# Unused bf16 matmuls in TensorE's idle stretches, one-hot tables with the tile innermost, and a first half of 256 tokens, in an attention and mixture-of-experts kernel

## The chip, the core and the metric

The kernel runs on one core of a Trainium2 chip. The metric is the device time of one execution in microseconds (us). Below, TensorE is also called PE (matmuls) and PEld (its weight loads), VectorE DVE, ScalarE ACT, GpSimd POOL and SyncE SP, as in the profile.

## What is computed

Three stages follow each other. Nothing but the attention result links the first to the second, and `x` links the second to the third.

```python
# 8 batches, 8 heads, 576 tokens, 64 wide: 4608 tokens of 512
kv  = einsum('bhsd,bhse->bhde', k, v)
out = einsum('bhsd,bhde->bhse', q, kv)
x   = out / sqrt(mean(out*out, -1) + 1e-6) * g_norm
# routing: 4608 tokens, 8 experts, 576 tokens each, best logit first
logits = x @ w_gate
for idx in argsort(-logits.flatten()):
    tok, e = idx // 8, idx % 8
    if assigned[tok] < 0 and counts[e] < 576:
        assigned[tok] = e; counts[e] += 1
x[mask_e] = relu(x[mask_e] @ w1[e]) @ w2[e]      # for each expert e
h = max(x @ m1, x @ m2, x @ m3); result = h @ w_out
```

## The kernel before, in words

**Attention** (lines 76 to 262 and the loop at L425). Four pairs of batches, `bp` 0 to 3. `load` (L80) issues the pair's inputs on SP's queue: `kt` and `vt` in two parts (token tiles 0 to 4, "a", and 5 to 8, "b"), then `qt`; for the first pair each part of k and v comes in two halves of 256 columns. `kv` (L169) multiplies k and v in float32 for four pairs of heads `hp`; a 128x128 float32 matmul leaves two records in the trace. `bd_t` and `bd_w` (L187, L194) build a block matrix that also carries the gate weights, and `o_tile` (L203) multiplies one tile of 128 queries by it; ACT takes the squares (L219) and copies the product to `y` (L220), DVE sums the squares (L221). `norm_a` and `norm_b` (L224, L231) make the norm and the logits `L` for three tiles at a time. `pre` (L302) turns the logits of all 9 tiles of a pair into the best expert `oh`, a key `H`, and a table `G` of key against 63 thresholds (L325); `pre_mm` (L333) counts with it on TensorE (L337).

**First route** (`phase(0)`, L636). `top_search` (L524) narrows a threshold seven times: 36 small matmuls count (L555), `narrow` (L526) sends the result to all partitions by one matmul (L531), and DVE builds the next table (L552). After it L716 sums the counts of each expert, `finish` (L568) numbers the chosen tokens: prefix sums (L572 to L581), then the position of each token as `hi` and `ri` (L595, L596), two one-hot tables `q` (L603) and `w` (L609), and W2, which is `q` times the partition's number (ACT, L605) and times the tile's number (POOL, L606). 36 matmuls (L615) over the tiles and four more (L629) give the list of tokens `IDX`. `gather` (L799) fetches their rows from DRAM in five tiles by POOL's queue, `trans` (L809) transposes a tile on TensorE and writes its high part by ACT (L821) and its low part by DVE (L822) to `X`.

**Experts** (loop at L881). Per expert: 8 blocks `f` of the first weight, each for two halves of 288 tokens (`hf`, HS), three matmuls per product (`mm3`, L826 to L828: high x high, low x high, high x low); then the second weight; then the third layer. `advance` (L785) loads the weights and splits them into `ring` (ACT L341, POOL L342). `tick` (L852) runs after each half: one piece of a decoder for the third layer's weights (DVE L368, L370; POOL L372, L386) while expert 0 runs, and one step of the next expert's route, so the routes of experts 1 to 7 (`phase(p)`, the same `finish`, a search on ACT and DVE at L484) run beside the matmuls. `drain` (L865) ends the route before the next gather.

The order on each engine is the order of the code (a manual schedule): an instruction that waits holds back all behind it on its engine.

Of the kernel before, what the change touches and what calls it, by code (L numbers as in the profile page):

```python
# [32 lines left out]
J0 = 63  # L33
# [3 lines left out]
def body(ctx: ExitStack, tc: tile.TileContext, qx, kx, vx, g, wg, w1, w2, w123, wo, out):  # L37
# [13 lines left out]
    SEL = consts.tile([32, 224], BF, name="SEL")  # L51
    iot18 = consts.tile([128, 18], BF, name="iot18")
    onec = consts.tile([128, NT], F32, name="onec")
# [3 lines left out]
    tri = consts.tile([128, 128], BF, name="tri")  # L57
    iot = consts.tile([128, 32], BF, name="iot")
    BM = consts.tile([96, 3, E], F32, name="BM")
# [44 lines left out]
    for s in range(2):  # L104
# [12 lines left out]
                   allow_small_or_imprecise_dtypes=True)  # L117
    nc.vector.tensor_copy(iot, d1[:, :32])
    nc.vector.tensor_copy(iot18, d1[:, :18])
    nc.gpsimd.memset(SEL, 0.0)  # L120
# [78 lines left out]

    Y = {}  # L200
    SS = {}

    def o_tile(c):  # L203
        bp, ci = divmod(c, TP)
        gi = ci % 3
        if gi == 0:
            Y[0] = aw.tile([128, 3, NH // 2, 144], F32, name="y", bufs=3)
            SS[0] = aw.tile([128, 3, NH], F32, name="ss")
        po = aps.tile([128, 2, 512], F32, name="o", bufs=2)
        o = int(ci >= CA)  # L210
        parts = [(0, 128, 0 if ci < 4 else 1)] if ci != 4 else [(0, 64, 0), (64, 128, 1)]
        for p0, p1, r in parts:
            for hp in range(NH // 2):
                nc.tensor.matmul(po[p0:p1, hp // 2, (hp % 2) * 144:(hp % 2) * 144 + 144],  # L214
                                 QT[bp, o][:, hp, (ci - o * CA) * 128 + p0:(ci - o * CA) * 128 + p1], BD[r][:, hp, :],
                                 start=True, stop=True)
        pv = po[:, :, 0:288].rearrange("p a (b x) -> p a b x", b=2)
        sq = aw.tile([128, 2, 2, 128], F32, name="sq", bufs=4)
        nc.scalar.activation(sq, pv[:, :, :, 0:128], AF.Square)  # L219
        nc.scalar.copy(Y[0][:, gi].rearrange("p (a b) x -> p a (b x)", a=2), po[:, :, 0:288])  # L220
        nc.vector.tensor_reduce(SS[0][:, gi], sq.rearrange("p a b (h d) -> p (a b h) d", d=D),  # L221
                                axis=AX, op=OP.add)
# [79 lines left out]
    def pre(c0, n):  # L302
# [9 lines left out]
        sf = aw.tile([128, n], F32, name="kf")  # L312
        G = aw.tile([128, n, J0], BF, name="G", bufs=2)
        nc.vector.tensor_reduce(best, V.rearrange("p e c -> p c e"), axis=AX, op=OP.max)
# [110 lines left out]
    for bp in range(NP):  # L425
# [15 lines left out]
        for ci in range(TP):  # L441
# [12 lines left out]
            if ci == 5:  # L454
                for _ in range(3):
                    norm_x()
        if bp == NP - 1:
            lds.close()
            w3p = ctx.enter_context(tc.tile_pool(name="w3p", bufs=1, side="right"))
            es = ExitStack()  # L460
            early = es.enter_context(tc.tile_pool(name="early", bufs=1, side="right"))
            for i in ORDER[:9]:
                load64(i)
            x_store(36)
        norm_b()
        pre(t0, TP)
        while XQ:
# [100 lines left out]
    def finish(p, A, TIE):  # L568
# [7 lines left out]
        yield  # L576
        yield
        po = rps.tile([128, 512], F32, name="rps")
        nc.tensor.matmul(po[:, 0:1], tri, tots[:, 0:1], start=True, stop=True)
        nc.tensor.matmul(po[:, 1:2], tri, tots[:, 1:2], start=True, stop=False)  # L580
        nc.tensor.matmul(po[:, 1:2], ones, tots[:, 0:1], start=False, stop=True)  # L581
        of = rt.tile([128, 3], F32, name="of")
        cm = rt.tile([128, NT], F32, name="cm")
# [13 lines left out]
        yield kp  # L597
        W2 = rt.tile([128, 36, 36], BF, name="W1", bufs=2).rearrange("p c (a b) -> p c a b", b=2)
        w = rt.tile([128, 36, 36], BF, name="W1", bufs=2)[:, :, 0:32]
        q = rt.tile([128, NT, 18], BF, name="q", tag="KT0")  # L600
        R = rt.tile([32, 20, 2], BF, name="R")
        nc.gpsimd.memset(R, 0.0)
        nc.vector.tensor_tensor(q, hi[:, :, None].to_broadcast([128, NT, 18]),  # L603
                                iot18[:, None, :].to_broadcast([128, NT, 18]), op=OP.is_equal)
        nc.scalar.activation(W2[:, :, :, 0], q, AF.Copy, scale=tp)  # L605
        nc.gpsimd.tensor_mul(W2[:, :, :, 1], q, iotc[:, :, None].to_broadcast([128, NT, 18]))  # L606
        yield
        for i in (0, 18):
            nc.vector.tensor_tensor(w[:, i:i + 18], ri[:, i:i + 18, None].to_broadcast([128, 18, 32]),  # L609
                                    iot[:, None, :].to_broadcast([128, 18, 32]), op=OP.is_equal)  # L610
            yield
        yield
# [5 lines left out]
        pv = pi[0:32, 0:36].rearrange("p (a b) -> p a b", b=2)  # L618
        if o:
# [257 lines left out]
    w_load()  # L877
    for c in range(3):
        trans(0, c)
    bg_piece(1)  # L880
    for p in range(E):  # L881
# [3 lines left out]
        for f in range(8):  # L885
# [7 lines left out]
            for hf in range(2):  # L893
                cs = slice(hf * HS, hf * HS + HS)
                if p == 0 and f == 0 and hf:
                    trans(0, 3)
                    trans(0, 4)
# [3 lines left out]
                for k in range(4):  # L901
                    mm3(ps[:, :HS], w, slice(k * 128, k * 128 + 128), X[:, k], cs, k == 0, k == 3)
                nc.scalar.activation(h[:, 0, cs], ps[:, :HS], AF.Relu)
                if p or f or hf:
                    tick(2)
                nc.vector.scalar_tensor_tensor(h[:, 1, cs], ps[:, :HS], 0.0, h[:, 0, cs],  # L906
                                               op0=OP.max, op1=OP.subtract)
# [117 lines left out]
```

## Time and profile before

| | us |
|---|---|
| median of 3 runs (lowest, highest) | 1288.56 (1285.23, 1289.71) |
| the profiled execution | 1291.65 |
| its span, first to last instruction | 1289.9 |
| TensorE busy with matmuls | 1206.7 (94%) |
| VectorE, ScalarE, GpSimd busy | 640.2, 491.6, 446.1 |
| mean granted TensorE clock | 0.963 |

The profiled execution is 3.1 us over the median. Slices of the span tell the stages: attention reaches to about 116 us, the first route to about 159 us, the first expert to about 323 us, and the other seven take some 138 us each. In a row of the timeline stand the start, the time from the first to the last of a group (in us), the engine, the line, the operation, output and inputs with shapes, and in brackets the idle time of the engine before it and what ended it. A matmul's duration contains its pipeline; how fast matmuls follow each other is read from starts.

### The profile page before, as it was taken

Reading aid. Unit: us, or ns where it says so; the run is one execution under the profiler, and the core shown is the slowest. Engines: PE = TensorE matmul, PEld = TensorE weight load, DVE = VectorE, ACT = ScalarE, POOL = GpSimd, SP = SyncE. Lnnn points to the kernel's source line nnn. Section 1 sums busy time; section 2 is a strip of 40 time slices with the busy share of each in tenths; the row PEclk is TensorE's granted clock in tenths of the full one; section 3 lists DMA queues with packets and bytes.
Section 4 is the critical chain, followed back from the end, with each engine's and each line's share of the span. In section 5 each row is a group of like instructions: output and inputs, shape, how many; then the busy total and the mean of one; then the engine's idle time right before and its main releaser. Section 6 shows DMA issues by size and latency. Waiting matters only on the chain.

```text
span 1289.9 us, 23164 instructions
## 1 busy us (share of the span) xinstructions
PE 1206.7 (94%) x8814; PEld 1143.6 (89%) x8814; DVE 640.2 (50%) x2017; ACT 491.6 (38%) x1214; POOL 446.1 (35%) x503
## 2 busy tenths in 40 slices
PE   7996386898999999999999999999999999999997
PEld 6886286888899989998999999998999899989995
DVE  2676559985466427652775157625763321122110
ACT  1556336752364125422552155314631331133110
POOL 0342158645531325132412352234213361134121
PEclk9998568898999999999999999999999999999998
DMA  9778722511330313121321133113302152013201
GB/s 327 301 274 334 281 75 83 180 50 58 108 114 26 99 27 122 66 75 47 109 75 58 42 116 98 58 42 96 110 32 69 53 165 94 2 50 123 66 1 41
DMA packets 52031, 133.63 MB, mean 104 GB/s; under 512 B 5840, under 2 KB 10448, under 8 KB 50384
## 3 DMA queue, kind: packets, MB, share of 16 engines
q1 hardware_dynamic: 44672, 109.07, 25.4%
q0 software_dynamic: 6944, 23.07, 5.3%
q8 instruction: 69, 1.13, 0.4%
q14 instruction: 42, 0.34, 0.1%
q10 hardware_dynamic: 304, 0.02, 0.0%
HBM read 110.12 MB, written 22.02 MB: 102 GB/s over the span
## 4 chain that ended last, share of the span: by engine, by line
PE 73%; DVE 13%; issue 5%; ACT 5%; POOL 2%; DMA 1%; POOLq 0%; ACTq 0%; SPq 0%; DVEq 0%
PE mm L826 18%; PE mm L827 17%; PE mm L828 17%; PE kv L179 4%; ACT W L492 3%; PE mm L971 3%; PE mm L973 3%; PE mm L972 3%; DVE T L512 3%; PE o L214 3%; PE tp L815 1%; DVE w L370 1%; DVE H L906 1%; PE rps L615 1%; DVE an L507 1%
## 5 line engine op out<-in xcount | busy, mean ns | idle before, releaser
L826 PE MATMUL mm<-X,w 128*128 128x288 f32 x1152 | 347.4, 302 | 0.0
L827 PE MATMUL mm<-X,w 128*128 128x288 f32 x1152 | 342.4, 297 | 5.0 <-POOL w L386 5.0
L828 PE MATMUL mm<-X,w 128*128 128x288 f32 x1152 | 341.8, 297 | 0.0
L342 POOL TENSOR_TENSOR ring<-raw,ring 128x512 fp32r<-128x512 f32 x128 | 167.8, 1313 | 244.5 <-ACT ring L341 228.4
L827 PEld LDWEIGHTS mm<-X,w 128*128 128x128 f32 x1152 | 218.3, 189 | 5.5 <-POOL w L386 5.5
L948 POOL TENSOR_TENSOR H<-t,H 128x288 fp32r<-128x288 f32 x96 | 78.8, 821 | 410.3 <-ACT H L947 410.2
L826 PEld LDWEIGHTS mm<-X,w 128*128 128x128 f32 x1152 | 218.5, 190 | 0.4
L828 PEld LDWEIGHTS mm<-X,w 128*128 128x128 f32 x1152 | 217.9, 189 | 0.0
L946 DVE TENSOR_TENSOR t<-mm,t 128x288 f32<-128x288 f32 x192 | 87.0, 453 | 171.6 <-PE mm L828 171.3
L826 PE MATMUL mm<-X,ring 128*128 128x288 f32 x512 | 157.2, 307 | 2.3 <-ACT X L821 1.3
L826 PE MATMUL mm<-H,ring 128*128 128x288 f32 x512 | 156.7, 306 | 0.0
L827 PE MATMUL mm<-X,ring 128*128 128x288 f32 x512 | 153.7, 300 | 0.8 <-POOL ring L342 0.8
L828 PE MATMUL mm<-X,ring 128*128 128x288 f32 x512 | 153.8, 300 | 0.0
L827 PE MATMUL mm<-H,ring 128*128 128x288 f32 x512 | 152.2, 297 | 0.0
L828 PE MATMUL mm<-H,ring 128*128 128x288 f32 x512 | 152.1, 297 | 0.0
L492 ACT ACTIVATE W<-KT,T 96x384 bf16<-96x384 f32 x168 | 102.1, 608 | 103.6 <-DVE T L512 103.5
L947 ACT CAST H<-t 128x288 fp32r<-128x288 f32 x96 | 41.3, 430 | 262.0 <-DVE t L946 262.0
L826 PEld LDWEIGHTS mm<-X,ring 128*128 128x128 f32 x512 | 99.2, 194 | 3.6 <-ACT X L821 2.1
L827 PEld LDWEIGHTS mm<-X,ring 128*128 128x128 f32 x512 | 98.9, 193 | 1.2 <-POOL ring L342 1.2
L828 PEld LDWEIGHTS mm<-X,ring 128*128 128x128 f32 x512 | 98.7, 193 | 0.3 <-DVE X L822 0.3
L826 PEld LDWEIGHTS mm<-H,ring 128*128 128x128 f32 x512 | 98.0, 191 | 0.0
L827 PEld LDWEIGHTS mm<-H,ring 128*128 128x128 f32 x512 | 97.5, 190 | 0.0
(246 smaller groups left out, 2055.1 us busy)
## 6 DMA issues: line engine op xcount, KB each, us to landing
raw<-w_dram SPq DMA_DIRECT2D x128, 256.0 KB, 2.7
ring<-wod SPq DMA_DIRECT2D x48, 512.0 KB, 3.5
xd<-xs SPq DMA_DIRECT2D x36, 256.0 KB, 6.2
w<-w_dram SPq DMA_DIRECT2D x18, 512.0 KB, 6.3
qta<-qx_dram SPq DMA_DIRECT2D x4, 1280.0 KB, 10.2
qtb<-qx_dram SPq DMA_DIRECT2D x4, 1024.0 KB, 8.9
kta<-kx_dram SPq DMA_DIRECT2D x3, 1280.0 KB
vta<-vx_dram SPq DMA_DIRECT2D x3, 1280.0 KB, 13.4
```

What stands on the lines that cost most here:

```text
L179: nc.tensor.matmul(KV[b][:, hp, :], KT[bp, o][p0:p1, c - o * CA, h], VT[bp, o][p0:p1, c - o * CA, h], start=(i == 0), stop=(i == len(cs) - 1))
L214: nc.tensor.matmul(po[p0:p1, hp // 2, (hp % 2) * 144:(hp % 2) * 144 + 144], QT[bp, o][:, hp, (ci - o * CA) * 128 + p0:(ci - o * CA) * 128 ...
L342: e.tensor_sub(lo, raw, hi)
L492: nc.scalar.activation(gs[:, j], KT, AF.Sign, bias=T[0:96, 1 + j:2 + j], scale=-1.0, accum_out=cnt[:, j:j + 1])
L512: nc.vector.tensor_scalar(Tn, nx, T[:, 0:1], tot, op0=OP.add, op1=OP.add)
L826: nc.tensor.matmul(ps, wt[:, 0, ws], x[:, 0, xs], start=first, stop=False)
L827: nc.tensor.matmul(ps, wt[:, 1, ws], x[:, 0, xs], start=False, stop=False)
L828: nc.tensor.matmul(ps, wt[:, 0, ws], x[:, 1, xs], start=False, stop=last)
L946: nc.vector.tensor_tensor(t2, ps[:, :HS], (t1, t1, t2)[j], op=OP.max)
L947: nc.scalar.copy(m[:, 0, cs], t2)
L948: nc.gpsimd.tensor_sub(m[:, 1, cs], t2, m[:, 0, cs])
L971: nc.tensor.matmul(pss[c], l[:, 0, ls], w[:, 0, :], start=(fc == 0), stop=False)
```

## The change

Four things are changed. (1) `heat(n, ps)` issues n matmuls of a zeroed 128x512 bf16 tile `warm`, whose products nothing reads: 26 ahead of the first `kv`; in the first route 2 after each of the seven broadcasts of `narrow`, 6 before L716, 6 before the prefix sums' matmuls, 10 behind them, and 18 behind L629: 80 in all. (2) At the end of the attention, `pre` runs for six tiles of the last pair ahead of the last two query tiles and for three after them (before: nine after them), and the copy of the product of the last tile but one goes behind the squares of the last. (3) In every route the tables are laid out with the tile innermost and made from bf16 copies `hb` of `hi` and `ri`; W2 is written by DVE alone; the matmuls of L615 then read columns that lie 36 elements apart. (4) The first block of expert 0 is cut into 256 and 320 tokens in place of 288 and 288, so its first part needs two transposed tiles; three are transposed behind it.

```diff
+    warm = consts.tile([128, 512], BF, name="warm")
+    nc.gpsimd.memset(warm, 0.0)
+    def heat(n, ps):
+        for _ in range(n):
+            nc.tensor.matmul(ps, warm[:, 0:128], warm, start=True, stop=True)
+    heat(26, aps.tile([128, NH // 2, 128], F32, name="bt").rearrange("p a b -> p (a b)"))
...
-    nc.vector.tensor_copy(iot, d1[:, :32])
-    nc.vector.tensor_copy(iot18, d1[:, :18])
+    nc.vector.tensor_copy(iotm, d1[:, 0:32, None].to_broadcast([128, 32, NT]))
...
-        nc.scalar.copy(Y[0][:, gi].rearrange("p (a b) x -> p a (b x)", a=2), po[:, :, 0:288])
+        YQ.append((Y[0][:, gi].rearrange("p (a b) x -> p a (b x)", a=2), po))
+        while YQ and c != NT - 2:
+            yt, pt = YQ.pop(0)
+            nc.scalar.copy(yt, pt[:, :, 0:288])
...
+            if c == NT - 3:
+                pre(t0, 6)
...
-        pre(t0, TP)
+        if bp == NP - 1:
+            pre(t0 + 6, 3)
+        else:
+            pre(t0, TP)
...
             nc.tensor.matmul(pb[:, 0:J], ones8, ex[:, 0:J], start=True, stop=True)
+            heat(2, aps.tile([128, 2, 512], F32, name="o", bufs=2)[:, 0])
...
         yield
+        if p == 0:
+            hp = ps1.tile([128, 4, 128], F32, name="tp").rearrange("p a b -> p (a b)")
+            heat(6, hp)
         po = rps.tile([128, 512], F32, name="rps")
...
+        if p == 0:
+            heat(10, hp)
...
-        nc.vector.tensor_tensor(q, hi[:, :, None].to_broadcast([128, NT, 18]),
-                                iot18[:, None, :].to_broadcast([128, NT, 18]), op=OP.is_equal)
-        nc.scalar.activation(W2[:, :, :, 0], q, AF.Copy, scale=tp)
-        nc.gpsimd.tensor_mul(W2[:, :, :, 1], q, iotc[:, :, None].to_broadcast([128, NT, 18]))
-        yield
-        for i in (0, 18):
-            nc.vector.tensor_tensor(w[:, i:i + 18], ri[:, i:i + 18, None].to_broadcast([128, 18, 32]),
-                                    iot[:, None, :].to_broadcast([128, 18, 32]), op=OP.is_equal)
-            yield
+        nc.vector.tensor_copy(hb[:, 0], hi)
+        nc.vector.tensor_copy(hb[:, 1], ri)
+        nc.vector.tensor_tensor(q, hb[:, 0:1].to_broadcast([128, 18, NT]), iotm[:, 0:18], op=OP.is_equal)
+        nc.vector.tensor_scalar(W2[:, 0], q, tp, None, op0=OP.mult)
+        nc.vector.tensor_mul(W2[:, 1], q, iotc[:, None, :].to_broadcast([128, 18, NT]))
+        yield
+        nc.vector.tensor_tensor(w, hb[:, 1:2].to_broadcast([128, 32, NT]), iotm, op=OP.is_equal)
+        yield
+        yield
         yield
...
-            nc.tensor.matmul(pi[0:32, 0:36], w[:, c, :], W2[:, c].rearrange("p a b -> p (a b)"),
+            nc.tensor.matmul(pi[0:32, 0:36], w[:, :, c], W2[:, :, :, c],
...
+        if p == 0:
+            heat(18, hp)
         IDX[p] = rt.tile([128, 5], I32, name="idx", bufs=3)
...
+        if p == 0:
+            heat(6, ps1.tile([128, 4, 128], F32, name="tp").rearrange("p a b -> p (a b)"))
         pc = rps.tile([128, 512], F32, name="rps")
...
-    for c in range(3):
+    for c in range(2):
         trans(0, c)
...
+                if p == 0 and f == 0:
+                    cs = slice(256, S) if hf else slice(0, 256)
+                sz = cs.stop - cs.start
                 if p == 0 and f == 0 and hf:
+                    trans(0, 2)
                     trans(0, 3)
```

Three places of the order are shown. In them L81 is `heat`, and L187, L198 and L223 of the changed kernel are L179, L190 and L214 of the kernel before.

TensorE at the start of the program, before:

```order
L1021 UNCONDITIONAL_BRANCH
L179 MATMUL kv<-vta,kta 128x128 x21
L179 MATMUL kv<-vtb,ktb 128x128 x4
L179 MATMUL kv<-vta,kta 128x128
L179 MATMUL kv<-vtb,ktb 128x128 x4
```

and now (26 pairs of weight load and matmul stand there; the last is shown):

```order
L1053 UNCONDITIONAL_BRANCH
...
L81 LDWEIGHTS warm
L81 MATMUL bt<-warm 128x512
L187 MATMUL kv<-vta,kta 128x128 x21
L187 MATMUL kv<-vtb,ktb 128x128 x4
L187 MATMUL kv<-vta,kta 128x128
```

The 26 pairs now stand ahead of the first product of k and v, and nothing behind them has moved.

VectorE at the end of the attention, before (`ss` are the sums of squares, `a` the norm's input, `best` and `G` belong to `pre`):

```order
L245 TENSOR_REDUCE L<-u 128x3x8
L221 TENSOR_REDUCE ss<-sq 128x8 x2
L226 TENSOR_SCALAR a<-ss 128x24
L236 RECIPROCAL r<-t 128x24
...
L245 TENSOR_REDUCE L<-u 128x3x8
L314 TENSOR_REDUCE best<-L 128x9
...
L325 TENSOR_TENSOR G<-H_202,th_143 128x567
```

and now:

```order
L257 TENSOR_REDUCE L<-u 128x3x8
L326 TENSOR_REDUCE best<-L 128x6
...
L337 TENSOR_TENSOR G<-H_229,th_170 128x378
L339 TENSOR_SCALAR k_1213<-k_1211 128x6
L340 TENSOR_SCALAR L_231<-k_1213 128x6
L233 TENSOR_REDUCE ss<-sq 128x8 x2
L238 TENSOR_SCALAR a<-ss 128x24
...
L326 TENSOR_REDUCE best<-L 128x3
...
L337 TENSOR_TENSOR G<-H_229,th_170 128x189
```

The thirteen instructions of `pre` are issued twice, the first time ahead of the last two sums of squares.

TensorE from the end of the first route to the second part of block 0 of expert 0, before (`xg` are gathered tiles):

```order
L629 MATMUL rps<-R,SEL 128x10
L815 MATMUL mm<-ident,xg_1818 128x128 x4
L815 MATMUL mm<-ident,xg_1820 128x128 x4
L815 MATMUL mm<-ident,xg_1822 128x128 x4
L826 MATMUL mm<-X,ring 128x288
...
L828 MATMUL mm<-X,ring 128x288
L815 MATMUL mm<-ident,xg_1824 128x128 x4
L815 MATMUL mm<-ident,xg_1826 128x128 x4
L826 MATMUL mm<-X,ring 128x288
```

and now (the 18 pairs end with the first two rows):

```order
L81 LDWEIGHTS warm
L81 MATMUL tp<-warm 128x512
L843 MATMUL mm<-ident,xg_1931 128x128 x4
L843 MATMUL mm<-ident,xg_1933 128x128 x4
L854 MATMUL mm<-X,ring 128x256
...
L856 MATMUL mm<-X,ring 128x256
L843 MATMUL mm<-ident,xg_1935 128x128 x4
L843 MATMUL mm<-ident,xg_1937 128x128 x4
L843 MATMUL mm<-ident,xg_1939 128x128 x4
L854 MATMUL mm<-X,ring 128x320
```

The third tile's transposes have moved behind the first twelve products, which are 256 columns wide, and the twelve behind them are 320 wide.

## Rows read from the trace of the kernel before

**Rows 1.** Timeline of TensorE, first and second pair of batches.

```profile
8.71 10.95 PE L179 MATMUL kv<-vta,kta 128*128 128x128 f32 x42 [8.71 <-DMA vta<-vx_dram]
...
28.20 1.15 PE L214 MATMUL o<-BD,qta 128*128 128x144 f32 x8
...
41.24 5.99 PE L179 MATMUL kv<-vta,kta 128*128 128x128 f32 x42
...
53.90 1.15 PE L214 MATMUL o<-BD,qta 128*128 128x144 f32 x8
```

**Rows 2.** Windows of TensorE: stretch, length, busy (instructions), granted clock, DMA share, GB/s.

```profile
9.00:10.00 1.00, 1.00 (x6) 1.00 1.09 373
...
119.00:120.00 1.00, 0.00 (x0) 0.63 1.02 397
...
180.00:181.00 1.00, 1.00 (x7) 0.65 0.00 0
```

**Rows 3.** Timeline of the start: a fill by POOL, the issue of the first queries.

```profile
1.40 0.28 POOL L120 MEMSET SEL<- 32x224 bf16 x1
...
11.11 1.34 SPq L96 DMA_DIRECT2D qta<-qx_dram  x1
```

**Rows 4.** The tile `qta` by itself: its transfers' time to landing.

```profile
DMA to landing us min/median/max: 10.2/10.2/10.2
```

**Rows 5.** Timeline of TensorE, last layer of expert 0: two matmuls of 512 columns.

```profile
320.19 0.40 PE L971 MATMUL mm<-ring,H 128*128 128x512 f32 x1
320.42 0.40 PE L972 MATMUL mm<-ring,H 128*128 128x512 f32 x1
```

**Rows 6.** Chain of waits at the end of the attention: start, us, engine, tile, line.

```profile
122.03 0.29 DVE best L314
...
123.44 0.76 DVE G L325
```

**Rows 7.** Timeline of the first route's end: search, counts of experts, prefix sums.

```profile
135.45 1.34 PE L555 MATMUL rps<-W,oh 128*8 128x15 bf16 x36 [0.93 <-DVE W L552]
...
142.88 0.17 PE L531 MATMUL rps<-ex,ones 8*128 8x15 bf16 x1 [0.25 <-DVE ex L528]
...
145.39 0.17 PE L716 MATMUL rps<-c,ones 128*128 128x16 bf16 x1 [2.34 <-DVE c L712]
...
147.85 0.19 PE L579 MATMUL rps<-tots,tri 128*128 128x1 bf16 x1 [2.29 <-DVE tots L574]
```

**Rows 8.** Timeline of the first route: a bf16 product, the one-hot table, the matmuls over it.

```profile
144.24 0.31 DVE L565 TENSOR_TENSOR g<-oh,gt 128x288 bf16<-128x288 bf16 x1
...
149.65 0.83 DVE L603 TENSOR_TENSOR q<-hi,iot 128x648 bf16<-128x648 int32 x1
...
152.34 1.34 PE L615 MATMUL rps<-W,W 128*32 128x36 bf16 x36 [4.18 <-POOL W L606]
```

**Rows 9.** Timeline of expert 0, blocks 0 and 1.

```profile
161.83 1.28 POOL L342 TENSOR_TENSOR ring<-raw,ring 128x512 fp32r<-128x512 f32 x1
...
164.02 0.61 PE L826 MATMUL mm<-X,ring 128*128 128x288 f32 x1 [0.78 <-ACT X L821]
...
169.84 0.61 PE L826 MATMUL mm<-X,ring 128*128 128x288 f32 x1 [0.56 <-ACT X L821]
...
172.71 0.44 PE L828 MATMUL mm<-X,ring 128*128 128x288 f32 x1
...
175.60 0.61 PE L827 MATMUL mm<-X,ring 128*128 128x288 f32 x1 [0.84 <-POOL ring L342]
```

**Rows 10.** Waits of TensorE, 120 to 300 us: line, waited for, us in total, times, longest.

```profile
PE rps L679 <- DVE V L675: 9.7, 2, 8.8
```

**Rows 11.** Weight loads of two lines: count, then ns min/median/max, first and last start.

```profile
L337 PEld LDWEIGHTS <-oh x36: 91/92/115, 62.2 to 124.6; 128*8 128x8 bf16 x36
...
L615 PEld LDWEIGHTS <-W x288: 92/93/113, 151.7 to 1038.5; 128*32 128x32 bf16 x144
```

**Rows 12.** Waits of TensorE, 280 to 320 us.

```profile
PE mm L827 <- POOL w L386: 5.0, 2, 3.3
```

More of the change, by code (lines that the diff above doesn't have):

```diff
@@ L51, in body @@
     SEL = consts.tile([32, 224], BF, name="SEL")
-    iot18 = consts.tile([128, 18], BF, name="iot18")
     onec = consts.tile([128, NT], F32, name="onec")
@@ L57, in body @@
     tri = consts.tile([128, 128], BF, name="tri")
-    iot = consts.tile([128, 32], BF, name="iot")
+    iotm = consts.tile([128, 32, NT], BF, name="iotm")
     BM = consts.tile([96, 3, E], F32, name="BM")
@@ L200, in body @@
     Y = {}
+    YQ = []
     SS = {}
@@ L312, in pre @@
         sf = aw.tile([128, n], F32, name="kf")
-        G = aw.tile([128, n, J0], BF, name="G", bufs=2)
+        G = aw.tile([128, TP, J0], BF, name="G", bufs=2)[:, 0:n]
         nc.vector.tensor_reduce(best, V.rearrange("p e c -> p c e"), axis=AX, op=OP.max)
@@ L597, in finish @@
         yield kp
-        W2 = rt.tile([128, 36, 36], BF, name="W1", bufs=2).rearrange("p c (a b) -> p c a b", b=2)
-        w = rt.tile([128, 36, 36], BF, name="W1", bufs=2)[:, :, 0:32]
-        q = rt.tile([128, NT, 18], BF, name="q", tag="KT0")
+        W2 = rt.tile([128, 36, 36], BF, name="W1", bufs=2).rearrange("p (b a) c -> p b a c", b=2)
+        w = rt.tile([128, 36, 36], BF, name="W1", bufs=2)[:, 0:32]
+        q = rt.tile([128, 18, NT], BF, name="q", tag="KT0")
+        hb = rt.tile([128, 2, NT], BF, name="hb")
         R = rt.tile([32, 20, 2], BF, name="R")
         nc.gpsimd.memset(R, 0.0)
-        nc.vector.tensor_tensor(q, hi[:, :, None].to_broadcast([128, NT, 18]),
-                                iot18[:, None, :].to_broadcast([128, NT, 18]), op=OP.is_equal)
-        nc.scalar.activation(W2[:, :, :, 0], q, AF.Copy, scale=tp)
-        nc.gpsimd.tensor_mul(W2[:, :, :, 1], q, iotc[:, :, None].to_broadcast([128, NT, 18]))
+        nc.vector.tensor_copy(hb[:, 0], hi)
[3 more added lines that the diff above has]
+        nc.vector.tensor_mul(W2[:, 1], q, iotc[:, None, :].to_broadcast([128, 18, NT]))
         yield
-        for i in (0, 18):
-            nc.vector.tensor_tensor(w[:, i:i + 18], ri[:, i:i + 18, None].to_broadcast([128, 18, 32]),
-                                    iot[:, None, :].to_broadcast([128, 18, 32]), op=OP.is_equal)
-            yield
+        nc.vector.tensor_tensor(w, hb[:, 1:2].to_broadcast([128, 32, NT]), iotm, op=OP.is_equal)
+        yield
+        yield
         yield
@@ L614, in finish @@
         for c in range(NT):
-            nc.tensor.matmul(pi[0:32, 0:36], w[:, c, :], W2[:, c].rearrange("p a b -> p (a b)"),
+            nc.tensor.matmul(pi[0:32, 0:36], w[:, :, c], W2[:, :, :, c],
                              start=(c == 0), stop=(c == NT - 1))
         o = 2 * (p % 2)
-        pv = pi[0:32, 0:36].rearrange("p (a b) -> p a b", b=2)
+        pv = pi[0:32, 0:36].rearrange("p (b a) -> p a b", b=2)
         if o:
@@ L901, in body @@
                 for k in range(4):
-                    mm3(ps[:, :HS], w, slice(k * 128, k * 128 + 128), X[:, k], cs, k == 0, k == 3)
-                nc.scalar.activation(h[:, 0, cs], ps[:, :HS], AF.Relu)
+                    mm3(ps[:, :sz], w, slice(k * 128, k * 128 + 128), X[:, k], cs, k == 0, k == 3)
+                nc.scalar.activation(h[:, 0, cs], ps[:, :sz], AF.Relu)
                 if p or f or hf:
                     tick(2)
-                nc.vector.scalar_tensor_tensor(h[:, 1, cs], ps[:, :HS], 0.0, h[:, 0, cs],
+                nc.vector.scalar_tensor_tensor(h[:, 1, cs], ps[:, :sz], 0.0, h[:, 0, cs],
                                                op0=OP.max, op1=OP.subtract)
```

## The prediction

> **What bounds the kernel now.** I began with the page's slices: TensorE (PE) is busy for 94% of the span, and the gaps lie in the first quarter. So I went through that quarter alone. First the timeline of PE at the start [rows 1]. The same 42 records take 10.95 us in the first pair of batches and 5.99 us in the second, a ratio of 1.83. No wait stands between them, so PE is the bound there, at half speed. The granted clock of that stretch is printed as 1.00 [rows 2], yet the durations are those of the low level (1.2 GHz); I go by the durations. Then the chain at the end of the attention [rows 6]: it runs on DVE, instruction after instruction, so PE is not the bound there. In the first route PE and DVE answer each other [rows 7, 8], at a granted clock that fell in the slice from 119 us, when PE stood idle, and rose in that from 180 us, when it had run without a pause since 175.60 [rows 2, 9]. So blocks 0 and 1 of expert 0 run at the low level. After them the bound changes again: PE waits 8.8 us at one point for DVE's V [rows 10].
>
> **The start of the attention.** 26 matmuls of 512 columns are added. The nearest rows are the 512-column matmuls of the last layer, 0.23 us apart at the high level [rows 5]; by 1.83 that is 0.43 us at the low one. So the 26 cost 6.1 us at best and 11.1 at worst. They can start when POOL has zeroed their tile: it filled 224 elements by 1.68 us [rows 3], so I estimate 1.5 us. With as long a run at the low level as ahead of the rise in rows 9 and 2, some 5 us, 12 go at 0.43 and 14 at 0.23, 8.4 us, and the first kv starts at 9.9 us in place of 8.71. From there the second pair shows what warm work costs: 53.90 - 41.24 = 12.66 us from the first kv to the first query tile [rows 1]. The first query tile then starts at 22.5 us in place of 28.20: **5.7 us gained**. It needs its queries: issued at 11.11, 10.2 us to landing [rows 3, 4], so there at 21.3, and 22.5 is kept. With no delay at all it could start at 21.4 (6.8 gained); if the matmuls stay at the low level to their end, the start moves to 12.6 and the warm stretch ends at 25.3 (2.9 gained). What follows is bound by PE and shifts as a whole, as each later load is issued when PE has released its buffer.
>
> **The end of the attention.** pre for nine tiles takes from 122.03 to 124.20 [rows 6], of which the table G is 0.76. Cut in six and three, its twelve extra instructions cost their fixed part again. Ten instructions lie between 122.03 and 123.44, 0.14 us apart; 12 x 0.14 = 1.7 at most, and since half of that is elements that only move, about 1.2. The first call stands ahead of the last two sums on an engine that the chain shows without a gap, so nothing hides it. Three counting matmuls instead of nine are then left, which gives some 0.2 back: **1.0 us lost** (0 to 1.7). The copy that goes behind a square I cost at nothing: DVE comes to those sums later than ACT makes the squares.
>
> **The first route.** In the search the two extra matmuls lie in a gap of 0.93 us [rows 7] and take 0.47 to 0.86, so they cost nothing, and gain nothing while the clock stays low, as I assume: the small matmuls left it low, and a gap for DVE stays in each round. Behind the last round stand 2 + 6 from 143.05 us on: 8 x 0.43 = 3.4, so L716 starts at 146.4 in place of 145.39, 1.0 lost. From 142.9 on PE now runs with hardly a pause, so I let the clock rise near 148. The next 6 end before L579 is due (147.85 + 1.0), the 10 at 0.23 end at 151.3, before the tables are ready. The tables: L565 does 288 bf16 elements in 0.31, G 567 of float32 in 0.76 [rows 8, 6]. That is 0.16 plus 1.04 ns an element for float32, and half of it for bf16. So q's 648 cost 0.50 (0.83 before), the second half of W2 0.50, w's 1152 0.76, the first half of W2 0.33 to 0.83, two copies 0.2 each. Issued one behind the other they take about 2.4 us against 2.69 from L603 to L615 [rows 8]: 0.3 gained (0.8 lost if all go at the slower rate). L615 takes 1.34 [rows 8], and 0.73 by the ratio if all of it follows the clock; I take 1.0, 0.3 gained. The 18 behind L629 take 4.2 us and end as the first gathered tile lands. Sum: **0.4 us lost** (2.0 lost to 2.0 gained).
>
> **Blocks 0 and 1 of expert 0.** The first product needs two tiles, but also ring's low part, which POOL ends at 161.83 + 1.28 = 163.11 behind its five gathers [rows 9]. So it starts 0.9 us earlier at most. Twelve matmuls took 2.87 / 11 x 12 = 3.1 us; at the high level and 256 columns, 1.5. Until the second half started, 2.7 us went by for two tiles; three at the high level I give the same. It starts at 163.1 + 1.5 + 2.7 = 167.3 in place of 169.84, needs 1.9 for 320 columns plus some 0.4 for the last low part, and ends at 169.6 in place of 172.95: 3.4 gained. Block 1 then waits for the ACT and POOL split as before, and its 5.0 us at the low level become 2.7: 2.3 gained. Sum: **5.7 us gained**, with no change 0. Behind it stands the wait on V of rows 10. DVE is the one waited for there, but its work in that stretch is set off by PE's halves, so I let the gain pass.
>
> **Later routes.** POOL loses one 648-element product per route and ACT one, DVE does less. It counts only in expert 0, where PE waits 5.0 us for POOL's decoder [rows 12]: **0.5 gained** (0 to 2). In the others the route lies beside PE's own work.
>
> **A rule against it.** L615 now reads its columns 36 elements (72 bytes) apart. The weight load of L337 already reads so, 8 columns, and takes 92 ns, like the 32 adjacent columns of L615 [rows 11]; by that the stride is free, and I charge nothing. The Trainium skill, SBUF — State Buffer, in its note on SBUF cachelines, says that each access which crosses to another 16-byte line pays a penalty, and that bf16 may be strided by 8 elements for free. By that rule every element of both operands would pay. What it would cost here is the last rival.
>
> **The sum**: -5.7 + 1.0 + 0.4 - 5.7 - 0.5 = -10.5 us, so 1281.1 against the profiled execution's 1291.65. That execution lies 3.1 us over the median of the runs; against the median, 1288.56 - 10.5 = **1278.0 us**.
>
> **The rivals.**
> - *DVE and POOL keep the end of V where it was relative to the route's end.* For it: the 8.8 us that PE stands there already [rows 10]. Against it: that work waits for PE's halves. Then the 5.7 of blocks 0 and 1 turn into a longer wait on V: 1283.7. Chance 0.18.
> - *The clock rises at the start but not in the route.* The small matmuls of 130 to 150 us never raised it, and the added ones leave gaps. Then L716's 1.0, 0.4 at the ten, 18 x 0.43 = 7.7 (2.9 us past the gathered tile) and 1.0 at the attention's end are lost, 5.7 and 1.3 at block 0 are gained: 1.7 gained, 1286.9. Chance 0.12.
> - *Slower: zeros that nothing reads don't raise the clock at all.* Place: the first kv. 26 x 0.43 = 11.1 us end at 12.6, so kv starts 3.9 later at the old speed; the route loses 1.0 + 0.4 + 2.9, the attention's end 1.0, block 0 gives 1.3 back: 7.9 lost, 1296.5. It decides if kv's 42 records still take over 10 us. For it: PE's own float32 work did not lift the durations for many us [rows 1]. Against it: dense work did lift the clock in rows 2. Chance 0.10.
> - *The stride costs.* If 36 pairs of load and matmul take twice as long, 1.0 us more in each of eight routes, 8 lost in all: 1286. The trace speaks against it as far as 8 columns go [rows 11]. Chance 0.06. The Trainium skill's rule on SBUF's lines, told above, is what asks for it.
>
> **How the numbers follow.** The forecast keeps 0.54. No change means within 0.3%, 3.9 us, which is about what a measurement can tell: 1284.7 to 1292.4. The forecast lies below it whole, the first rival mostly (0.13 of 0.18), the second and the fourth in it but for 0.03: faster 0.70, same 0.20, slower 0.10. The range: best ends of all terms at once (6.8, 0, 2.0, 6, 2) make 17, seldom together, so I go to 15 gained, 1273; above it takes in the first rival and the second at 1287. Outside are the slower rival and a little at either end.
>
> **What would show it.** Right: 42 kv records in about 6 us, from about 10 us on; the first query tile near 22.5; the attention's last G about 4.5 to 5 us earlier, not 5.7; the granted clock high before the gather; twelve products of block 0 in 1.5 us; V's wait still near 9 us. Wrong: 42 records over 10 us; a granted clock of 0.50 between 150 and 160; a wait on V of 14 us; L615's matmuls over 40 ns apart at the high level.

## The result and the profile after

The changed kernel takes 1296.64 us in the median of 4 runs (1295.76 to 1299.07), the kernel before 1287.2 beside it: the ratio is 1.0075, interval 1.005 to 1.0101. It is **slower by 9.4 us** where 10.5 less were forecast, and lies outside the range. The profiled execution takes 1295.89 us, its span 1294.1. The ratios with their 95% intervals are worked out from the single runs beside each other, so they are not always the quotient of the medians.

Timeline of TensorE at the start, after (L81 is `heat`, L187 `kv`, L223 `o_tile`):

```profile
1.34 7.43 PE L81 MATMUL bt<-warm 128*128 128x512 bf16 x26 [1.34 <-POOL warm L76]
9.35 3.05 PE L187 MATMUL kv<-vta,kta 128*128 128x128 f32 x20 [0.57 <-DMA vta<-vx_dram]
13.10 3.06 PE L187 MATMUL kv<-vta,kta 128*128 128x128 f32 x22 [0.70 <-DMA vta<-vx_dram]
...
22.83 1.15 PE L223 MATMUL o<-BD,qta 128*128 128x144 f32 x8
```

The unused matmuls end at 8.8 us. The 42 records then take 3.05 + 3.06 us of work, like the second pair of before [rows 1], and PE now waits twice for `vta`: here the load is the bound. The first query tile starts at 22.83 in place of 28.20, 5.4 us earlier; 5.7 were forecast.

Timeline of VectorE, after: the last table `G` of the attention, then the tables of the first route (`q`, W2 by `tp`, W2 by tile, `w`):

```profile
119.70 0.36 DVE L337 TENSOR_TENSOR G<-H,th 128x189 bf16<-128x189 f32 x1
...
146.20 0.50 DVE L629 TENSOR_TENSOR q<-hb,iotm 128x648 bf16<-128x648 bf16 x1
146.73 0.39 DVE L630 TENSOR_SCALAR W<-q,tp 128x648 bf16<-128x648 bf16 x1
147.04 0.49 DVE L631 TENSOR_TENSOR W<-q,iotc 128x648 bf16<-128x648 bf16 x1
147.44 0.75 DVE L633 TENSOR_TENSOR W<-hb,iotm 128x1152 bf16<-128x1152 bf16 x1
```

`G` ends at 120.06. From the first query tile that is 97.2 us, and 96.0 before [rows 1, 6]: the split of `pre` costs 1.2. The tables take 0.50, 0.39, 0.49 and 0.75, where 0.50, 0.33 to 0.83, 0.50 and 0.76 were worked out.

Timeline of TensorE, first route and blocks 0 and 1, after (L744 was L716, L600 L579, L639 L615, L843 L815, L854 to L856 the three products, L705 the reading of V):

```profile
139.60 2.25 PE L81 MATMUL tp<-warm 128*128 128x512 bf16 x6 [0.48 <-PE rps L548]
141.69 0.17 PE L744 MATMUL rps<-c,ones 128*128 128x16 bf16 x1
...
144.18 0.18 PE L600 MATMUL rps<-tots,tri 128*128 128x1 bf16 x1 [0.81 <-DVE tots L592]
...
148.25 2.59 PE L639 MATMUL rps<-W,W 128*32 128x36 bf16 x36 [1.58 <-DVE W L633]
...
151.67 5.43 PE L81 MATMUL tp<-warm 128*128 128x512 bf16 x17 [0.25 <-issue]
...
159.20 0.38 PE L854 MATMUL mm<-X,ring 128*128 128x256 f32 x1 [0.78 <-ACT X L849]
...
169.94 0.40 PE L855 MATMUL mm<-X,ring 128*128 128x288 f32 x1 [1.07 <-POOL ring L354]
...
199.61 0.66 PE L705 MATMUL rps<-ident,V 128*96 128x128 f32 x2 [8.88 <-DVE V L701]
```

Windows of TensorE there, after (columns as in [rows 2], with the weight loads, VectorE, ScalarE and GpSimd between PE and the clock):

```profile
141.00:142.00 1.00, 0.95 (x6) 0.38 (x4) 0.07 (x1) 0.00 (x0) 0.00 (x0) 0.88 0.99 393
...
152.00:153.00 1.00, 1.00 (x4) 0.35 (x3) 0.00 (x0) 0.00 (x0) 0.14 (x1) 0.50 0.00 0
155.00:156.00 1.00, 1.00 (x6) 0.49 (x5) 0.00 (x0) 0.00 (x0) 0.70 (x2) 1.00 0.49 193
```

The clock rose at 141 us, during the six matmuls ahead of L744, earlier than forecast; it fell at 151 to 152, behind the pause and the 36 matmuls of the route, and rose again under the 18; it falls there in e7 below too, whose reads are adjacent. Blocks 0 and 1 run mostly at the high level. But one row stands out: **L639 takes 2.59 us at the high clock**, where L615 took 1.34 at the low one [rows 8]. It does so in every route. The chain of waits, before:

```profile
312.37 1.00 PE rps L615 x36
...
1037.66 1.00 PE rps L615 x36
```

and after:

```profile
304.90 2.52 PE rps L639 x36
...
1039.40 2.52 PE rps L639 x36
```

These are the second and the eighth route. The changed kernel was 7.5 us ahead at the second and is 1.7 behind at the eighth: 9.2 lost in six intervals. Five of these lose 1.2 to 1.5 us each, and one group of 36 takes 1.52 longer; the third, from the fourth group to the fifth, loses 2.7. The durations of single instructions in L639, after:

```profile
L639 PEld LDWEIGHTS <-W x288: 133/138/158, 148.2 to 1041.6; 128*32 128x32 bf16 x144
L639 PE MATMUL rps<-W,W x288: 244/247/260, 148.2 to 1041.7; 128*32 128x36 bf16 x144
```

A weight load takes 138 ns, and 92 or 93 before [rows 11].

That third interval holds a second loss, which follows such a group. TensorE in the fourth route, after, beside expert 3's work:

```profile
565.10 2.59 PE L639 MATMUL rps<-W,W 128*32 128x36 bf16 x36
...
568.28 0.44 PE L854 MATMUL mm<-X,w 128*128 128x288 f32 x1
...
571.52 0.29 PE L854 MATMUL mm<-X,w 128*128 128x288 f32 x1
```

and windows behind the eighth, after:

```profile
1042.00:1043.00 1.00, 1.00 (x6) 1.00 (x7) 0.61 (x3) 0.00 (x0) 0.89 (x1) 0.68 0.18 61
1043.00:1044.00 1.00, 1.00 (x6) 1.00 (x5) 0.00 (x0) 0.00 (x0) 0.00 (x0) 0.50 0.92 340
...
1046.00:1047.00 1.00, 1.00 (x10) 1.00 (x9) 0.00 (x0) 0.00 (x0) 0.70 (x2) 1.00 0.05 16
```

The profile shows PE busy without a pause, yet the granted clock goes to 0.50 for some three us and products take 0.44 in place of 0.29; 3.4 us at half speed would cost 1.7 (an estimate from the windows). It happened behind the fourth and the eighth group here, and behind the same two in the variant with the strided tables alone (e2). In the twelve kept traces whose routes read adjacent columns (the kernel before and its variants) no fall begins behind any of the seven later groups. Windows of the kernel before, behind its fourth group (it starts at 570.05):

```profile
571.00:572.00 1.00, 1.00 (x12) 0.96 (x9) 0.61 (x3) 0.00 (x0) 0.00 (x0) 1.00 0.00 0
572.00:573.00 1.00, 1.00 (x11) 0.84 (x10) 0.00 (x0) 0.00 (x0) 0.00 (x0) 1.00 0.00 0
```

Waits of TensorE, after, 280 to 320 us, and then 120 to 300 us:

```profile
PE mm L855 <- POOL w L398: 5.0, 2, 3.3
```

```profile
PE rps L705 <- DVE V L701: 9.4, 2, 8.9
```

Both stand as before [rows 12, 10]: the 0.5 forecast at the wait on `w` did not come, nor did the wait on V grow.

### The profile page after: what moved, and what is told of

Its sections match the earlier page's. It is cut to its first block, busy times and chain, and to the rows that moved or that the text cites. A ratio compares the mean times of both kernels' runs of the same rounds, so it can differ in the third digit from the quotient of the medians.

```text
span 1294.1 us, 23333 instructions
## 1 busy us (share of the span) xinstructions
PE 1230.1 (95%) x8889; PEld 1152.3 (89%) x8894; DVE 638.7 (49%) x2053; ACT 484.2 (37%) x1206; POOL 432.3 (33%) x496
## 4 chain that ended last, share of the span: by engine, by line
PE 74%; DVE 13%; ACT 5%; issue 5%; POOL 2%; DMA 1%; SPq 0%; POOLq 0%; ACTq 0%; DVEq 0%
PE mm L854 18%; PE mm L855 17%; PE mm L856 17%; PE kv L187 3%; ACT W L509 3%; PE mm L1003 3%; PE mm L1005 3%; PE mm L1004 3%; DVE T L529 3%; PE o L223 3%; PE rps L639 2%; PE tp L843 1%; DVE H L938 1%; DMA vta<-vx_dram 1%; DVE w L382 1%
## 5 line engine op out<-in xcount | busy, mean ns | idle before, releaser
L854 PE MATMUL mm<-X,w 128*128 128x288 f32 x1152 | 347.0, 301 | 0.0
L856 PE MATMUL mm<-X,w 128*128 128x288 f32 x1152 | 340.7, 296 | 0.0
L854 PEld LDWEIGHTS mm<-X,w 128*128 128x128 f32 x1152 | 218.5, 190 | 0.8
L856 PEld LDWEIGHTS mm<-X,w 128*128 128x128 f32 x1152 | 218.4, 190 | 0.0
L854 PE MATMUL mm<-X,ring 128*128 128x288 f32 (+1 forms) x512 | 155.5, 304 | 2.4 <-ACT X L849 1.3
L854 PE MATMUL mm<-H,ring 128*128 128x288 f32 x512 | 157.0, 307 | 0.0
L855 PE MATMUL mm<-X,ring 128*128 128x288 f32 (+1 forms) x512 | 152.1, 297 | 1.9 <-POOL ring L354 1.9
L856 PE MATMUL mm<-H,ring 128*128 128x288 f32 x512 | 152.7, 298 | 0.0
L856 PE MATMUL mm<-X,ring 128*128 128x288 f32 (+1 forms) x512 | 152.2, 297 | 0.0
L854 PEld LDWEIGHTS mm<-X,ring 128*128 128x128 f32 x512 | 97.6, 191 | 3.4 <-ACT X L849 2.0
L854 PEld LDWEIGHTS mm<-H,ring 128*128 128x128 f32 x512 | 98.5, 192 | 1.1 <-issue 1.1
L855 PEld LDWEIGHTS mm<-X,ring 128*128 128x128 f32 x512 | 97.3, 190 | 2.3 <-POOL ring L354 2.3
L855 PEld LDWEIGHTS mm<-H,ring 128*128 128x128 f32 x512 | 97.9, 191 | 0.0
L856 PEld LDWEIGHTS mm<-H,ring 128*128 128x128 f32 x512 | 97.7, 191 | 0.0
```

What stands on the lines that cost most here:

```text
L854: nc.tensor.matmul(ps, wt[:, 0, ws], x[:, 0, xs], start=first, stop=False)
L855: nc.tensor.matmul(ps, wt[:, 1, ws], x[:, 0, xs], start=False, stop=False)
L856: nc.tensor.matmul(ps, wt[:, 0, ws], x[:, 1, xs], start=False, stop=last)
```

## The experiments

Two theories were put for the loss: the strided reads of TensorE cost it, or VectorE's additional work in each route does. For the small gain: the first stretch of the kernel before differs from execution to execution, and the forecast read it from a slow one. Medians and ratios are against the kernel before, run beside each.

**e1: the tables as before, the rest of the change kept.**

```diff
-            nc.tensor.matmul(pi[0:32, 0:36], w[:, :, c], W2[:, :, :, c],
+            nc.tensor.matmul(pi[0:32, 0:36], w[:, c, :], W2[:, c].rearrange("p a b -> p (a b)"),
...
+        nc.scalar.activation(W2[:, :, :, 0], q, AF.Copy, scale=tp)
+        nc.gpsimd.tensor_mul(W2[:, :, :, 1], q, iotc[:, :, None].to_broadcast([128, NT, 18]))
```

> The change with its tables undone: q, w and W2 as before (tile outermost, W2 from ScalarE and GpSimd), all else of the change kept. Theory S, the stride: the 36 matmuls over the tables cost 2.52 us per later route against 1.00 and 2.61 against 1.35 in the first, 1.52 x 7 + 1.26 = 11.9 us; undone, and with 0.4 us lost on the slower tables of the first route, the time falls by about 11.5 from the changed kernel's 1296.6 to 1285, a ratio to the kernel before of 0.993 to 1.001; the 36 matmuls take 1.0 again. Theory R, the loss is elsewhere (VectorE's added W2 work delays the evictions that the matmuls wait for, or the added matmuls delay something late): the ratio stays over 1.004 even if the 36 matmuls are quick again.

1286.0 us (12 runs), ratio 0.9987 (0.997 to 1.0004); the 36 matmuls take 1.00 again. So the loss lies in part 3 of the change: by the ratios it costs 0.9%, some 11.3 us, and the rest gains 1.7, hardly measurable.

**e2: the new tables alone, on the kernel before.** The hunks on `iotm`, `W2`, `w`, `q`, `hb` and the matmuls of the change, and nothing else.

> The kernel before with the new tables alone (bf16, tile innermost, W2 by VectorE, strided reads by the 36 matmuls), nothing else of the change. S: 11.9 us lost less 0.4 in the first route: 1287.2 + 11.5 = 1298.7, a ratio of 1.007 to 1.011. R: under 1.004.

1302.45 us (4 runs), ratio 1.0119 (1.0086 to 1.0152): part 3 costs 11 to 20 us, in the median more than the 11.5 expected. Each later group takes 2.52 or 2.53. The profiled run is the fastest of the four (granted clock 0.967 on average); the other three are 3 to 8 us slower at 0.957 to 0.962, and what happened in them no trace shows.

**e3: the stride by itself.** Groups of 36 unused pairs at the start of the kernel before, ten 512-column matmuls between them; the first number is the step of the 32 loaded columns, the second that of the 36 streamed ones.

```diff
+    for a, b in ((1,1), (36,1), (1,36), (36,36), (2,2), (4,4), (8,8), (16,16)):
+        for _ in range(36):
+            nc.tensor.matmul(sp[0:32, 0:36], ap_of(32, a), ap_of(36, b), start=True, stop=True)
+        heat(10, sp)
```

> The kernel before with, ahead of its first product, 26 unread bf16 matmuls of 512 columns and eight groups of 36 unread matmuls of the tables' shape (32 columns loaded, 36 streamed), ten wide ones behind each group. The groups differ in the distance of the elements read: load and stream adjacent; load 36 apart; stream 36 apart; both 36 apart; both 2, 4, 8, 16 apart. S: adjacent takes about 1.0 us per group (28 ns a pair), both 36 apart about 2.5 (70 ns), with the cost on one or both operands, and distances between show where it sets in; a price by 16-byte lines would leave 2 and 4 nearly free and 8, 16 and 36 alike. R: all groups alike within 0.2 us. The time of the whole rises by some 30 us, which tells nothing.

Timeline of TensorE in e3, in the order of that list (without the last):

```profile
8.46 1.07 PE L94 MATMUL bt<-strd 128*32 128x36 bf16 x36
...
11.73 2.29 PE L97 MATMUL bt<-strd 128*32 128x36 bf16 x36
...
16.21 2.56 PE L100 MATMUL bt<-strd 128*32 128x36 bf16 x36
...
20.97 2.59 PE L103 MATMUL bt<-strd 128*32 128x36 bf16 x36
...
25.75 1.07 PE L106 MATMUL bt<-strd 128*32 128x36 bf16 x36
...
29.01 1.47 PE L109 MATMUL bt<-strd 128*32 128x36 bf16 x36
...
32.68 2.60 PE L112 MATMUL bt<-strd 128*32 128x36 bf16 x36
```

Either operand alone, 36 elements apart, takes a group from 1.07 to 2.29 or 2.56 us, both together to 2.59: they run beside each other, and the longer one counts. Two elements apart (4 bytes) is free, four take 1.47, eight (16 bytes) the full price, and sixteen 2.67. The Trainium skill, SBUF — State Buffer, in its note on SBUF cachelines, says bf16 may be strided by 8 elements for free; here a step of 8 costs as much as one of 36, and the measurement decides. Its other half, that a penalty is paid for each access that crosses to another 16-byte line, agrees in that steps of 8, 16 and 36 cost about alike. The granted clock stays at 1.00 through all these groups, so a fall does not follow every strided group.

**e7: VectorE's bf16 tables, but stored so that TensorE reads neighbours.** Everything else as in the change.

```diff
-        nc.vector.tensor_scalar(W2[:, 0], q, tp, None, op0=OP.mult)
+        nc.vector.tensor_scalar(W2[:, :, :, 0], q, tp, None, op0=OP.mult)
...
-            nc.tensor.matmul(pi[0:32, 0:36], w[:, :, c], W2[:, :, :, c],
+            nc.tensor.matmul(pi[0:32, 0:36], w[:, c, :], W2[:, c].rearrange("p a b -> p (a b)"),
```

> The change with its bf16 tables and W2 on VectorE alone, but laid out as before, the table's entries innermost, so the 36 matmuls read adjacent columns (for W2 VectorE writes every second element). Theory S: the stride alone costs, so this runs as e1_old_tables, 1286 within 2, and the 36 matmuls take 1.0 us. Rival: VectorE's added work costs part of it: 1289 or more.

1284.04 us (10 runs), ratio 0.9978 (0.9963 to 0.9992). VectorE's tables now take 0.83, 0.60, 0.86 and 1.34 in the first route, longer than in the change, and still the kernel is 12.6 us faster than the changed one (1296.64 - 1284.04; 12.5 by the ratios). Its 36 matmuls in the first route:

```profile
150.51 1.07 PE L643 MATMUL rps<-W,W 128*32 128x36 bf16 x36 [3.04 <-DVE W L636]
```

So the stride is the loss, and VectorE's work is not. From the second group to the eighth e7 needs 724.15 us, the change 734.50: 10.35 more, of which 6 x 1.52 = 9.1 are the groups. Interval by interval it is 1.2, 1.5, 3.0 and three times 1.6; the 3.0 is the interval with the fall of the clock, so that fall costs some 1.4.

**e10: why the trace of before did not show it.** As e3, with other numbers of columns.

```diff
+    for n, a, m, b in ((8,1,36,1), (8,36,36,1), (16,36,36,1), (24,36,36,1), (32,36,36,1),
+                       (32,1,9,1), (32,1,9,36), (32,1,18,36), (32,1,27,36), (8,1,63,1), (8,36,63,1)):
+        for _ in range(36):
+            nc.tensor.matmul(sp[0:n, 0:m], ap_of(n, a), ap_of(m, b), start=True, stop=True)
+        heat(10, sp)
```

> The kernel before with unused matmuls at its start, in groups of 36 pairs of weight load and matmul, ten 512-column matmuls between them; a group differs only in how many columns are loaded and streamed, and whether these lie next to each other or 36 apart. Theory: a column that lies 36 apart takes some 1.86 ns (59 ns between pairs with 32 loaded columns, 67 with 36 streamed ones, in the earlier groups), load and stream run beside each other, and a pair takes the longer of the two but not under some 25 ns (36 adjacent). Then, 36 streamed adjacent: 8 loaded 36 apart 1.07 us as with 8 adjacent, 16 some 1.25, 24 some 1.8, 32 2.29; 32 loaded adjacent: 9 streamed 36 apart about as 9 adjacent, 18 some 1.35, 27 some 1.95. 8 loaded 36 apart with 63 streamed adjacent, the form of the table of thresholds: as with 8 adjacent. Rival: each strided operand costs a fixed amount per instruction: then 8 loaded 36 apart take about 2.2 us as well, and 9 streamed some 2.4.

Timeline of TensorE in e10: 8 columns loaded adjacent, then 8, 16 and 24 loaded 36 apart, 36 streamed adjacent:

```profile
8.58 1.06 PE L94 MATMUL bt<-strd 128*8 128x36 bf16 x36
...
11.83 1.07 PE L97 MATMUL bt<-strd 128*8 128x36 bf16 x36
...
15.09 1.29 PE L100 MATMUL bt<-strd 128*16 128x36 bf16 x36
...
18.57 1.79 PE L103 MATMUL bt<-strd 128*24 128x36 bf16 x36
```

and the weight loads of the first two groups, one line each:

```profile
L94 PEld LDWEIGHTS <-strd x36: 82/83/85, 8.6 to 9.4; 128*8 128x8 bf16 x36
```

```profile
L97 PEld LDWEIGHTS <-strd x36: 91/92/100, 11.8 to 12.7; 128*8 128x8 bf16 x36
```

32 loaded took 2.29 again; 9, 18 and 27 columns streamed 36 apart took 1.12, 1.37 and 2.08; with 63 streamed, 8 loaded adjacent took 1.21 and 8 loaded 36 apart 1.22. So each column that lies 36 apart takes some 1.9 ns (59 ns between pairs with 32 of them loaded, 67 with 36 streamed), and it is hidden until the sum is longer than what the pair takes anyway, 25 ns in the first group ((1.06 - 0.18) / 35). Only the 27 streamed columns were a little dearer than expected (2.08 for 1.95). The rival, a fixed price per instruction, falls.

**e4: e1 without the split of `pre`.**

```diff
-            if c == NT - 3:
-                pre(t0, 6)
```

> As e1_old_tables, and pre for the last pair is one call for nine tiles again, and the copy of the last tile but one stands where it was. My theory: VectorE is full at the attention's end, and the last G came 1.2 us later for the split; without it 1.2 us faster than e1_old_tables, a ratio of 0.992 to 1.000. Rival: the split hides six tiles' work, and without it the time is the same or up to 1 us more.

1285.93 us (12 runs), ratio 0.9976 (0.996 to 0.9992), and 1286.0 with the split. In the traces it takes 95.7 us from the first query tile to the end of `G`, and 97.2 with the split: 1.5 lost there, too little for the runs to tell.

**e5: the 26 matmuls at the start alone, on the kernel before.**

```diff
+    heat(26, aps.tile([128, NH // 2, 128], F32, name="bt").rearrange("p a b -> p (a b)"))
```

> The kernel before with the 26 matmuls at the start alone. Theory V, the start varies: in the profiled execution of the kernel before the low level lasted to about 24 us and the first query tile started at 28.20, but in that of e2_only_tables, whose start has no added matmul either, the 42 kv records took 8.10 us and the tile started at 23.51. If executions without the matmuls lie between these, the matmuls gain 0.7 to 6 us each time and 2 to 3 in the median: a ratio of 0.997 to 0.999, and a first query tile at 22 to 23.5. Theory F, my forecast: 5.4 us in every execution, a ratio of 0.996 or less.

1283.96 us (12 runs), ratio 0.9974 (0.9959 to 0.9989): 3.3 us gained (1.4 to 5.3). That is in theory V's range; the 5.4 of theory F lies just outside the interval.

**e6: as e4, without the 54 matmuls of the first route.** Left of the change are the start and the first half of 256 tokens.

```diff
-        if p == 0:
-            heat(18, hp)
```

> As e4_no_pre_split without the 54 added matmuls of the first route: what stays of the change are the 26 at the start and the first part of 256 tokens. If the clock of blocks 0 and 1 is worth what I forecast, this is 4 to 5 us slower than e4_no_pre_split (1285.9 there): 1290, a ratio of 1.000 to 1.003. Rival: the clock lost in the route is mostly taken back by the wait on V behind block 7, and the time is within 1.5 us of e4_no_pre_split.

1282.76 us (12 runs), ratio 0.9976 (0.9962 to 0.9991): the 4 to 5 us expected did not come. It is no worse than e4, so the 54 gain nothing that can be measured, and the ratio lies where that of e5 does, so neither does the half of 256 tokens.

**e9: the 54 matmuls of the first route alone, on the kernel before.** All hunks of `heat` but the one at the start.

> The kernel before with the 54 unused matmuls of the first route's search and route alone; no matmuls at the start, no 256-token half, no other edit. If what they win in blocks 0 and 1 goes into the wait on V: within 1.5 us of the kernel before (1287), blocks 0 and 1 at the high clock, the wait on V longer by about what they won. Rival, the forecast's own term: blocks 0 and 1 are 3 to 5.7 us shorter and the end follows, 1282 to 1284. Second rival, they delay the route on DVE more than they win: 1288 to 1290.

1287.42 us (12 runs), ratio 1.0001 (0.9986 to 1.0016): nothing, though blocks 0 and 1 do run mostly at the high clock (1.00 in the window 160 to 170 us, 0.83 in the next). Between the end of `G` and the first gather 32.7 us go by, and 31.4 before. The first theory's time came, but not its place: the wait on V stays at 8.8.

**b1, b2: the kernel before, two more executions.**

> The kernel before once more, for a second profiled execution. Theory V: its first query tile starts at another time than 28.20 us, between 23.5 and 28.2, and its span is shorter than 1289.9 by that difference. Theory F: 28.2 within 0.5.

> The kernel before, unchanged, one more execution, to see how much the first stretch differs by itself. If the time at which the clock rises at the start differs from one execution to the next: the 42 kv records take anything from 8.0 to 11.0 us and the first query tile starts between 23.5 and 28.2 us, with a total that need not follow. Rival, the first stretch is a property of the kernel: one of the two values seen (10.95 us and 28.20, or 8.17 and 24.61) again within 0.2.

Timeline of TensorE, first pair, in b1 and then in b2:

```profile
9.77 8.17 PE L179 MATMUL kv<-vta,kta 128*128 128x128 f32 x42 [9.77 <-DMA vta<-vx_dram]
```

```profile
8.45 8.18 PE L179 MATMUL kv<-vta,kta 128*128 128x128 f32 x42 [8.45 <-DMA vta<-vx_dram]
```

8.17 and 8.18 us, where the execution ahead of the prediction took 10.95 [rows 1]; e2 and e9, which have no `heat` at the start either, took 8.10 and 10.36. The first query tile starts at 24.61 and 23.31, in e2 and e9 at 23.51 and 25.59; with `heat` at the start it lies between 22.05 and 23.29 in seven kernels. So theory V has the tile right, and neither of the rival's two values covers e9. V's other half fails: b1's span is 5.2 us shorter (1284.6), and the tile only 3.6 earlier. Another 1.9 lie between the end of `G` and V (81.3 against 83.2), as the clock of blocks 0 and 1 differs as well. Windows of the kernel before in the execution shown first, and in b2:

```profile
160.00:170.00 10.00, 7.94 (x31) 6.15 (x29) 3.86 (x7) 3.64 (x6) 2.79 (x3) 0.50 0.37 106
170.00:180.00 10.00, 8.16 (x31) 7.45 (x32) 3.39 (x12) 2.35 (x5) 3.64 (x3) 0.50 0.19 54
```

```profile
160.00:170.00 10.00, 6.97 (x35) 6.03 (x36) 3.78 (x13) 2.90 (x6) 3.08 (x3) 0.84 0.03 10
170.00:180.00 10.00, 10.00 (x66) 10.00 (x65) 5.45 (x8) 4.96 (x11) 6.35 (x6) 0.83 0.32 105
```

In b2 the clock rises at 163 us without any added matmul.

**e8: the start, the half of 256 tokens and e7's tables together.** No `heat` in the route, `pre` in one piece.

> The 26 matmuls at the start, the first half of 256 tokens, and the route's tables compared in bf16 on DVE but stored so that TensorE reads neighbouring columns; no matmuls in the route, pre in one piece. If only the stride hurt and VectorE's tables are good by themselves: not above the variant with the old tables (1282.76 us), some 1280 to 1282.5, since the same tables made the whole change 2.0 us faster than the old ones did (1284.04 against 1286.0). Rival, the tables on DVE delay V in expert 0, as DVE is the engine waited for there: 1283 to 1285, V's first use over 200 us.

1283.58 us (12 runs), ratio 0.9967 (0.9954 to 0.9979). Level with e5 and e6 within the intervals, and faster than both kernels. The 1280 to 1282.5 expected was missed, and the rival has the time but not its sign: V is first read at 198.6.

## Why the prediction was wrong

Stations in us, from the traces:

| | before (shown) | before (b2) | after |
|---|---|---|---|
| first query tile starts | 28.20 | 23.31 | 22.83 |
| end of the last `G` | 124.20 | 119.28 | 120.06 |
| first gather issued | 155.62 | 150.72 | 152.86 |
| first product of block 0 | 164.02 | 158.96 | 159.20 |
| V is read | 207.44 | 200.41 | 199.61 |
| first matmul of the last layer, expert 0 | 320.19 | 316.20 | 314.20 |
| end of the span | 1289.9 | 1285.8 | 1294.1 |

- **The step that failed is "by that the stride is free, and I charge nothing".** It held a load of 8 columns 36 apart against one of 32 adjacent, both 92 ns. e10 has the right comparison: 8 adjacent take 83, so the 92 did contain the stride. Beside 63 streamed columns it is 93 against 88, and there it is hidden: 1.22 against 1.21 for a group. With 32 loaded and 36 streamed columns nothing hides it. Charged right, the reads cost 1.52 us in each of eight routes, 12.2 in all, and more where the clock falls behind a group. The prediction's own sign for this came: L639's matmuls are 67 ns apart at the high level, where 40 was the limit. The last rival had the mechanism and a chance of 0.06, with 1.0 a route; its 1286 came from adding that to a sum that was itself too low.
- **The start.** The mechanism came as told: the records took 6.1 us of work and the first query tile came 5.4 earlier than in the execution it was read from. The size did not carry over to the median. The length of the slow stretch differs from execution to execution, and the sum took the full 5.7 off the median although the profiled execution lay 3.1 over it; e5 measured 3.3 alone. The Trainium skill, TensorE: Matmul & The Clock Gate, Part 1, says that the number of slow matmuls at a start varies between runs of one kernel; the five first stretches without `heat`, 8.10 to 10.95 us, agree.
- **Attention's end**: 1.0 lost was forecast, 1.2 came (1.5 between e1 and e4). Right.
- **The first route**: from the end of `G` to the gather 32.8 us against 31.4, 1.4 lost for 0.4, and the strided group alone is 1.25 longer than before (2.59 - 1.34). The tables' durations were right, and the clock rose earlier than told. It did not stay high until the gather, as the prediction had asked: it stands at 0.50 when the gather is issued.
- **Blocks 0 and 1**: from the gather to V 46.75 us against 51.82, 5.1 gained for 5.7. But it is 49.69 in b2 and 49.87 in b1, so against other executions 2.9 to 3.1; and in e9, from the end of `G` to V, 80.6 us go by against 81.1 and 81.3 there, so with the longer route little is left of it. This term too was read from one execution whose clock stayed low. The first rival's place, the wait on V, is not where it went: that wait is 8.9 as before.
- **Later routes**: 0.5 was forecast for a POOL product less; the wait on `w` stays at 5.0.
- **The slower rival** gave 1296.5, and 1296.64 came, by another cause: its condition, kv's records over 10 us, did not hold. A time that fits is no evidence for a mechanism.

Up to the last layer of expert 0 the changed kernel is 6.0 us ahead of the execution shown before, with 2.8 already spent on two strided groups; but it is only 2.0 ahead of b2 and 0.5 ahead of b1. From there on it loses 10.2: six groups of 1.52, 9.1, and two falls of the clock at some 1.4, which would make 11.9. Why it is 1.7 less stays open; from the second group to the end, the twelve kept traces with adjacent reads themselves lie between 975.7 and 978.2 us. What a fall takes is read by comparing intervals, here and with e7; no run took it away alone, and why the clock falls there stays open.

The miss as a whole, 9.4 lost for 10.5 gained, is 19.9 us. By e1, some 11.3 of it are part 3; the rest of the change was to gain 9 to 10 of the 10.5, and gains 1.7 there. By the stations that shortfall lies mostly in the start and in blocks 0 and 1, both read from one slow execution.

## What to carry to other kernels

Compare a strided read with an adjacent one of the same number of columns, and ask what the pair of load and matmul hides; when a layout that suits VectorE is read column by column on TensorE, price the read at the strided rate, for every time it runs. A gain that rests on where the clock stands in one execution is a gain on that execution: look at the spread of the runs before taking it off the median. Unused matmuls paid here where PE's own speed was the bound, at the start, and not where other engines set the pace, in the route.

## What was not expected of the hardware

A bf16 step of 2 elements cost nothing, 4 cost 37% of a group (1.47 for 1.07), and 8 as much as 36. Groups of strided matmuls, with PE busy throughout, were followed by a fall of the granted clock from 1.00 to 0.50 behind two of seven later groups, in both kernels that have them, and behind none in the twelve traces whose routes read adjacent columns; the same groups in e3, with ten wide matmuls behind each, left it at 1.00. And the clock at the start and in blocks 0 and 1 of one unchanged kernel stood at different levels in different executions, worth 4.9 us at the first query tile.
